# Even heads' row moves through GpSimd's queue for twenty steps, batch 0's attention result kept in float32, and a row tile cleared by ScalarE

## The chip, the cores and the metric

The kernel runs on one core of one Trainium2 chip. The metric is the time of one execution in device microseconds. The engines are called as the profile calls them: PE is TensorE (matrix products; PEld is its weight load), DVE is VectorE, ACT is ScalarE, POOL is GpSimd, and SP is SyncE, which issues transfers. ACT and POOL can issue transfers too; a queue with a q (SPq, ACTq) is the issuing side.

## The reference

Attention with a mix over the heads before and after the softmax, then two feed-forward blocks. All in float32.

```python
batch, n_heads, seq, head_dim = (4, 12, 448, 64)
scores = scale * np.matmul(q, k.transpose(0, 1, 3, 2))
scores = np.einsum('bhij,hg->bgij', scores, w_pre)        # premix over heads
attn = softmax(scores)                                    # max, exp, sum, divide
attn = np.einsum('bhij,hg->bgij', attn, w_post)           # postmix over heads
x = np.matmul(attn, v)    -> 1792 tokens x 768
h = (x @ w1) * (x @ w2) @ w3 @ w_out                      # first block, d_ff 1024
g = np.maximum(0.01 * (h @ w_in), h @ w_in) @ w_out2      # second block, d_ff 2048
```

## The kernel before

The attention takes the first 360 us or so of the span, the two feed-forward blocks the rest. Each batch is cut into four chunks of queries (120, 120, 120 and 88 of them), and the chunks are worked through in `order`; batch 0 begins with its short chunk. A chunk is six pairs of heads for `qk` (L248) and five or six groups of up to twenty queries for everything behind it; there are 92 groups.

`qk` makes the scores of one pair of heads with queries on the partitions. To mix over heads, heads must be on the partitions: each head's scores are evicted from PSUM to a tile `s` (L260 on DVE, L262 on ACT) and then *moved* by a DMA from SBUF to SBUF (`move`, L274), which deals the 120 partitions to ten partitions (one per query of a block, twelve heads apart) and twelve columns of a row tile `rows_of`, name `sr`. There are three row tiles, used in turn, one per chunk. `premix` (L306) multiplies a row tile by `kpre` into `pm`, so it needs the moves of all twelve heads of its chunk. DVE takes the row maximum `mx` (L316), ACT the exponential `e` with the row sums `sm` (L323), `weigh` scales up to four blocks of `e` by 1/sum (L339: three by POOL, one by DVE; in the last steps L337: three by ACT, one by POOL), `postmix` (L360) writes `po`, DVE transposes it to `ap` (L375), and `av` (L392) multiplies by v into `px`, which ACT copies to `y` (L403). For batches 0 and 1, `y` is split in an upper half (`hi_act`, L72: a copy rounded to float32r) and a lower half (L405, POOL: the difference), and both are stored to `scr`. For batches 2 and 3 `y` is stored in float32 alone.

The loop runs in steps of two groups, k = 0, 2, ... 92, under a manual schedule: each engine takes its instructions in program order. Before the loop, eleven `qk` run early (the whole first chunk and five pairs of the second), with `turn` as filler products on PE. There, even heads are evicted by ACT, but those of odd pairs of the first chunk by DVE; the first chunk's even heads are moved by ACT's queue, everything else by SP's. In step k the pairs of groups ten (later eleven and twelve) ahead are made by `qk`, so the last pair of the second, third and fourth chunk is made in step 0, 6 and 12 and its premix stands at the end of step 2, 8 and 14; from the fifth chunk on there are two or three steps between. SP also issues the loads of q, k and v, in program order with the moves.

The row tiles are cleared once at the start (L151 by DVE, L155 by POOL), since `kpre` has zero rows that meet unused partitions.

The *seam* is a generator of the feed-forward part that the last steps of attention call: it loads the first weights and x (both batches' upper and lower halves, four transfers, L757), converts the first weight tile `wr` to `wc` and its halves `ws` in pieces (L100 to L111), and makes the first products `pm` (L587) while the last `av` still runs. Behind it the feed-forward blocks run on PE without gaps. The lower halves of x come in at the second of each pair of `pm`'s first twelve terms.

Of the kernel before, what the change touches and what calls it, by code (L numbers as in the profile page):

```python
# [22 lines left out]
def attention_moe_kernel(ctx: ExitStack, tc, qt, kt, vt, w_pre, w_post, w1, w2, w3t, w_out, w_in2, w_out2, out):  # L23
# [15 lines left out]
    P = 128  # L39
    JP = 112  # L40
    NJ = S // JP
    IB = 10
    LEAD, AT, SKIP = 10, (16, 20), 4
    CH = qt.shape[-1]
# [7 lines left out]
    while i0 < S:  # L52
# [4 lines left out]
    scr = [  # L57
        dram.tile([2, P, NPAIR, S], F32, name=f"scr_{b}") if b < 2 else dram.tile([P, NPAIR, S], F32, name=f"scr_{b}")
        for b in range(B)
# [58 lines left out]
    def attention(seam):  # L118
        with ExitStack() as es, ExitStack() as left:
# [30 lines left out]
            def constants_load():  # L150
                nc.vector.memset(rows_of[0], 0.0)  # L151
                for t in (kpre, kpost):
                    nc.gpsimd.memset(t, 0.0)
                for i in (1, 2):
                    nc.gpsimd.memset(rows_of[i], 0.0)  # L155
                for n, w in enumerate((w_pre, w_post)):
                    nc.sync.dma_start(out=wrep[:, n, :], in_=w)
# [69 lines left out]
            def qk(b, c, p, early=False):  # L227
# [29 lines left out]
                def out():  # L257
                    for e in range(2):
                        if early and (e or (b, c) == order[0] and p % 2):
                            nc.vector.tensor_copy(t[:m, e, :], pq[e][:m])  # L260
                        else:
                            nc.scalar.activation(out=t[:m, e, :], in_=pq[e][:m], func=ACTF.Copy)  # L262
                    for e in range(2):
                        args = srt[b, c], t[:m, e, :], 2 * p + e
                        move(*args, nc.sync if e or (b, c) != order[0] else nc.scalar)

# [8 lines left out]

            evs, staged = [], []

# [99 lines left out]
            def av(b, c, p):  # L377
# [21 lines left out]
                def out():  # L399
                    hi, lo = (y[:, i, 2 * g:2 * g + 2, :ni] for i in range(2))  # L400
                    if b < 2:
                        hi_act(hi, px[:, :, :ni])
                    nc.scalar.copy(lo.bitcast(F32), px[:, :, :ni])  # L403
                    if b < 2:
                        nc.gpsimd.tensor_tensor(out=lo, in0=lo.bitcast(F32), in1=hi.bitcast(F32), op=ALU.subtract)  # L405
# [3 lines left out]
                if p == NPAIR - 1:  # L409
                    if b < 2:  # L410
                        later.extend((scr[b][i, :, :, c0:c0 + ni], y[:, i, :, :ni].bitcast(F32)) for i in range(2))
# [85 lines left out]
            for k in range(0, NG + 2, 2):  # L497
# [8 lines left out]
                before = ets.pop(k - 2, None)  # L506
                ahead = [x for g in made[k] for x in slot(g)]
                for x in ahead:
                    qk(*x)
# [14 lines left out]
                if drain:  # L524
                    if old:
                        turns = postmix(old, before, now=False)
                        turn_out(turns.pop(0))
                    if k > LAST:
                        next(seam, None)
                    if now:  # L530
                        weigh(fresh, sm, ets[k], True)
                    while turns:
                        turn_out(turns.pop(0))
                else:
                    weigh(fresh, sm, ets[k], False)
                while lows:
                    lows.pop(0)()
# [26 lines left out]
    def moe():  # L564
# [66 lines left out]
        def first_half():  # L631
            with ExitStack() as er:
# [112 lines left out]
                def seam():  # L745
# [8 lines left out]
                    pos[0] += 1  # L754
                    for n in range(2):
                        for i in range(2):
                            nc.sync.dma_start(out=x[:, :, i, n * S:(n + 1) * S].bitcast(F32), in_=scr[n][i])  # L757
                    fill()
                    yield
                    steps = converting(cv, loaded.pop(0), (KM, P))  # L760
# [3 lines left out]
                    next(steps)  # L764
                    yield
                    try:
# [5 lines left out]
                    hi_act(w[:, 0], cf)  # L772
                    yield
                    lo_dve(w[:, 1], cf, w[:, 0])
# [347 lines left out]
```

## Time and profile before

| | us |
|---|---|
| three runs | 3006.95, 1218.69, 1223.53 |
| median | 1223.53 |
| profiled execution | 1220.24 |
| its span, first to last instruction | 1218.5 |
| mean granted clock of PE | 0.997 |

The page gives, for the span, the busy time of each engine, the busy share in forty slices, the chain of work that ended last, the costliest groups of instructions and the transfers. A clock of 1.00 is PE's upper level, 2.4 GHz; less is a mean over a stretch that was partly at 1.2 GHz. DMA share is the mean over the core's 16 DMA engines. A number in square brackets with an arrow is the time that an engine was idle before an instruction, and what ended it; where the wait was for several things, only one is named, and not always the right one.

### The profile page before, as it was taken

The numbers are of one execution on the slowest core, as the hardware profiler recorded it, in microseconds if no ns is written. First come the engines' busy times: TensorE is split into PE (matmuls) and PEld (weight loads), VectorE is DVE, ScalarE is ACT, GpSimd is POOL, SyncE is SP. The second block draws the span as 40 slices with busy tenths as digits, with TensorE's granted clock in tenths as the row PEclk, the third lists the DMA queues.
The fourth block names the chain that finished last, engine by engine and source line by source line (L and its number), as shares of the span: only waits on it lengthen the run. The fifth ranks groups of instructions, "written<-read, shape, count | busy, mean of one in ns | idle before, by whom it ended". The sixth has DMA issues, their size and how long they took to land.

```text
span 1218.5 us, 22377 instructions
## 1 busy us (share of the span) xinstructions
PE 1197.1 (98%) x8782; PEld 985.3 (81%) x8782; DVE 885.8 (73%) x1538; ACT 550.8 (45%) x1120; POOL 206.8 (17%) x160
## 2 busy tenths in 40 slices
PE   8899999999999999999999999999999999999998
PEld 5245555554478999998899999999999999999998
DVE  6677887888889998547795867667776657376572
ACT  3677777766755454323454342352233433322120
POOL 4566767666310000000000000000000000000000
PEclk9999999999999999999999999999999999999999
DMA  6876776756957756489674636063242221212012
GB/s 212 222 201 192 211 231 183 221 168 184 300 160 256 238 187 198 162 275 352 221 238 145 216 96 208 26 221 115 92 129 70 65 70 52 72 33 72 26 53 91
DMA packets 134282, 196.81 MB, mean 162 GB/s; under 512 B 26304, under 2 KB 114976, under 8 KB 134176
## 3 DMA queue, kind: packets, MB, share of 16 engines
q1 hardware_dynamic: 129656, 192.77, 49.7%
q10 hardware_dynamic: 4520, 2.61, 0.7%
q8 instruction: 69, 1.13, 0.4%
q14 instruction: 37, 0.30, 0.1%
HBM read 114.57 MB, written 42.07 MB: 129 GB/s over the span
## 4 chain that ended last, share of the span: by engine, by line
PE 82%; DVE 8%; DMA 5%; ACT 3%; issue 1%; ACTq 0%; SPq 0%; POOL 0%; DVEq 0%; POOLq 0%
PE pm L587 29%; PE po L601 19%; PE pp L898 17%; DVE ap L375 6%; PE pw L659 6%; PE px L392 5%; PE po L360 3%; ACT e L323 3%; DMA sr<-s 3%; PE pq L248 2%; DVE mx L316 1%; DMA x<-scr 1%; PE pm L306 1%; DMA q<-in_q_dram 1%; PE turn L293 1%
## 5 line engine op out<-in xcount | busy, mean ns | idle before, releaser
L587 PE MATMUL pm<-x,ws 128*128 128x384 f32 (+1 forms) x1152 | 233.9, 364 | 0.0
L587 PEld LDWEIGHTS pm<-x,ws 128*128 128x128 f32 x1152 | 208.7, 188 | 24.5 <-issue 0.6
L339 POOL TENSOR_SCALAR e<-e,sm 128x448 f32<-128x448 f32 x126 | 181.9, 1456 | 141.0 <-DVE sm L333 123.1
L323 ACT ACTIVATE e<-pm,mx 128x448 f32<-128x448 f32 x180 | 111.7, 632 | 85.3 <-DVE mx L316 80.8
L375 DVE STREAM_TRANSPOSE ap<-po 128x512 f32<-128x512 f32 (+3 forms) x228 | 116.7, 571 | 25.2 <-PE po L360 24.5
L898 PE MATMUL pp<-t,w 128*128 128x448 f32 x576 | 124.5, 368 | 0.0
L601 PE MATMUL po<-ws,g 128*128 128x384 f32 x672 | 117.2, 334 | 0.0
L601 PE MATMUL po<-wo,g 128*128 128x384 f32 x672 | 117.1, 334 | 0.0
L898 PEld LDWEIGHTS pp<-t,w 128*128 128x128 f32 x576 | 108.1, 188 | 10.9
L601 PEld LDWEIGHTS po<-wo,g 128*128 128x128 f32 x672 | 116.6, 188 | 0.2
L601 PEld LDWEIGHTS po<-ws,g 128*128 128x128 f32 x672 | 116.6, 188 | 0.0
L316 DVE TENSOR_REDUCE mx<-pm 128x1 f32<-128x448 f32 x180 | 98.5, 603 | 11.7 <-PE pm L306 11.7
L100 ACT ACTIVATE wc<-wr 128x768 f32<-128x768 f32 (+1 forms) x72 | 61.6, 858 | 85.0 <-DMA wr<-in_moe_w_dram 29.1
L392 PEld LDWEIGHTS px<-ap,vs 96*64 96x64 f32 (+1 forms) x1536 | 77.7, 136 | 22.1 <-ACT e L323 16.7
L898 PE MATMUL pp<-b,w 128*128 128x448 f32 x432 | 95.5, 368 | 0.0
L608 DVE TENSOR_TENSOR acc<-po,acc 128x384 f32<-128x384 f32 x84 | 45.5, 555 | 66.5 <-PE po L601 66.4
L306 PE MATMUL pm<-sr,kpre 64*64 64x448 f32 x720 | 82.0, 555 | 9.0 <-DMA sr<-s 4.8
L392 PE MATMUL px<-ap,vs 96*64 96x120 f32 (+3 forms) x1536 | 87.6, 266 | 2.9 <-ACT e L323 1.0
L360 PE MATMUL po<-e,kpost 64*32 64x512 f32 (+1 forms) x1472 | 89.1, 586 | 0.8 <-POOL e L339 0.7
L262 ACT ACTIVATE s<-pq 120x448 f32<-120x448 f32 (+1 forms) x178 | 82.2, 563 | 12.7 <-PE pq L248 10.9
L898 PEld LDWEIGHTS pp<-b,w 128*128 128x128 f32 x432 | 81.1, 188 | 8.0
L248 PEld LDWEIGHTS pq<-k,q 64*120 64x120 f32 (+1 forms) x528 | 44.6, 176 | 46.9 <-DVE ap L375 17.6
(104 smaller groups left out, 1580.9 us busy)
## 6 DMA issues: line engine op xcount, KB each, us to landing
sr<-s SPq DMA_DIRECT2D x144, 210.0 KB
wr<-in_moe_w_out_dram SPq DMA_DIRECT2D x24, 768.0 KB
wr<-in_moe_w_dram SPq DMA_DIRECT2D x16, 768.0 KB
wr<-in_moe_w_in_dram SPq DMA_DIRECT2D x16, 768.0 KB
wr<-in_moe_w_dram SPq DMA_DIRECT2D x16, 512.0 KB
sr<-s SPq DMA_DIRECT2D x42, 157.5 KB
vs<-in_v_dram SPq DMA_DIRECT2D x12, 512.0 KB
kept_w<-wc SPq DMA_DIRECT2D x16, 384.0 KB
```

Of the source, the lines that this page charges most:

```text
L262: nc.scalar.activation(out=t[:m, e, :], in_=pq[e][:m], func=ACTF.Copy)
L306: nc.tensor.matmul(pms[ns[s % len(ns)]][half:half + Q], kpre[rows], sr[rows, 2 * t + g, :], start=True, stop=True,)
L316: nc.vector.tensor_reduce(out=mxs[n], in_=pms[n], axis=AX.X, op=ALU.max, negate=True)
L323: ends["act"] = nc.scalar.activation(out=e[:, i], in_=pms.pop(n), func=ACTF.Exp, bias=mxs.pop(n), scale=1.0, accum_out=sm[:, i:i + 1])
L339: ends["dve" if eng is nc.vector else "pool"] = eng.tensor_scalar(out=e[:, i], in0=e[:, i], scalar1=rc[:, i:i + 1], scalar2=None, op0=ALU.mult
L360: nc.tensor.matmul(po[g][32 * r:32 * (r + 1), :m], kpost[rows, x], e[rows, :m, JS[r]:JS[r] + P], start=True, stop=True,)
L375: ends["dve"] = nc.vector.transpose(out=dst, in_=po[g][:, i0:i1])
L392: nc.tensor.matmul(px[e * D:(e + 1) * D, r, :nw].rearrange("p (n i) -> p n i", i=HQ), vs[rows, p, jc, e, :], ap[rows, x, :ns, jc, h * HQ:( ...
L587: nc.tensor.matmul(dst, wt[:, a, kk, :], x[kk][:, c, c0:c0 + w], start=(i == 0), stop=(i == len(steps) - 1))
L601: nc.tensor.matmul(po, g[m][:, a, t * P:(t + 1) * P], wts[m][:, c, cs], start=(m == 0 and j == 0), stop=(m == FQ - 1 and j == 2),)
L659: nc.tensor.matmul(pw, wt[:, x, kk, :], wos[kk][y][:, cs], start=(kk == 0 and j == 0), stop=(kk == KF - 1 and j == 2),)
L898: nc.tensor.matmul(dst, w[:, i, a, kk, :], b[:, kk, c, :], start=(kk == 0 and j == 0), stop=(kk == KH - 1 and j == 2),)
```

## The change

Even heads (e = 0) are always evicted by ACT in the early `qk`, odd ones by DVE. The early even heads are moved by POOL's queue. In the steps below k = 40, twenty of them, the even heads' moves are put on a list and issued by POOL's queue behind its part of `weigh`; odd heads stay on SP, and from step 40 on SP moves all. Batch 0's `y` is stored once in float32; at the seam it is loaded into the place of x's lower half, ACT copies it to the upper half in three pieces of 2 x 448 columns (two in the step of group 88, one in the next), and POOL subtracts behind its `weigh`. One of the two row tiles that POOL cleared is cleared by ACT, as a copy of the zeroed `kpre`.

```diff
-    LEAD, AT, SKIP = 10, (16, 20), 4
+    LEAD, AT, SOFT, SKIP = 10, (16, 20), 40, 4
...
-        dram.tile([2, P, NPAIR, S], ...) if b < 2 else dram.tile([P, NPAIR, S], ...)
+        dram.tile([2, P, NPAIR, S], ...) if b == 1 else dram.tile([P, NPAIR, S], ...)
...
-                for i in (1, 2):
-                    nc.gpsimd.memset(rows_of[i], 0.0)
+                nc.gpsimd.memset(rows_of[1], 0.0)
+                none = rows_of[2].rearrange("p n s -> p (n s)").rearrange("p (a b) -> p a b", b=Q)
+                nc.scalar.activation(
+                    out=none, in_=kpre.unsqueeze(1).to_broadcast([P, CH // IB * S // Q, Q]), func=ACTF.Copy
+                )
...
-                        if early and (e or (b, c) == order[0] and p % 2):
+                        if early and e:
                             nc.vector.tensor_copy(t[:m, e, :], pq[e][:m])
                         else:
                             nc.scalar.activation(out=t[:m, e, :], in_=pq[e][:m], func=ACTF.Copy)
                     for e in range(2):
                         args = srt[b, c], t[:m, e, :], 2 * p + e
-                        move(*args, nc.sync if e or (b, c) != order[0] else nc.scalar)
+                        if early or e or not soft[0]:
+                            move(*args, nc.sync if e or not early else nc.gpsimd)
+                        else:
+                            soon.append(args)
...
-                    if b < 2:
+                    if b == 1:
                         hi_act(hi, px[:, :, :ni])
                     nc.scalar.copy(lo.bitcast(F32), px[:, :, :ni])
-                    if b < 2:
+                    if b == 1:
                         nc.gpsimd.tensor_tensor(out=lo, in0=lo.bitcast(F32), in1=hi.bitcast(F32), op=ALU.subtract)
...
+                soft[0] = k < SOFT
...
-                    if k > LAST:
-                        next(seam, None)
+                    rest = next(seam, None) if k > LAST else None
                     if now:
                         weigh(fresh, sm, ets[k], True)
+                    if rest:
+                        rest()
...
                     weigh(fresh, sm, ets[k], False)
+                    while soon:
+                        move(*soon.pop(0), nc.gpsimd)
...
-                    for n in range(2):
-                        for i in range(2):
-                            nc.sync.dma_start(out=x[:, :, i, n * S:(n + 1) * S].bitcast(F32), in_=scr[n][i])
+                    for i, c0, src in ((1, 0, scr[0]), (0, S, scr[1][0]), (1, S, scr[1][1])):
+                        nc.sync.dma_start(out=x[:, :, i, c0:c0 + S].bitcast(F32), in_=src)
                     fill()
+                    def halves(*ks):
+                        hi, lo = ([x[:, k:k + 2, i, :S] for k in ks] for i in range(2))
+                        for y, z in zip(hi, lo):
+                            hi_act(y, z.bitcast(F32))
+                        def rest():
+                            for y, z in zip(hi, lo):
+                                nc.gpsimd.tensor_tensor(
+                                    out=z, in0=z.bitcast(F32), in1=y.bitcast(F32), op=ALU.subtract
+                                )
+                        return rest
                     yield
...
                     next(steps)
-                    yield
+                    yield halves(0, 2)
+                    rest = halves(4)
...
                     hi_act(w[:, 0], cf)
-                    yield
+                    yield rest
                     lo_dve(w[:, 1], cf, w[:, 0])
```

## Rows read from the trace of the kernel before

**Rows 1.** Stages: window, us, busy us (instructions) per engine, clock, DMA share, GB/s

```profile
84.00:312.00 228.00, 223.73 (x2990) 121.18 (x2992) 184.51 (x401) 165.89 (x466) 150.64 (x116) 1.00 0.69 199
38.00:42.00 4.00, 4.00 (x31) 1.40 (x39) 1.48 (x4) 3.03 (x8) 1.38 (x1) 0.64 0.92 217
80.00:84.00 4.00, 2.09 (x10) 0.72 (x12) 2.07 (x5) 1.34 (x4) 2.77 (x3) 0.73 0.66 196
```

**Rows 2.** Timeline of PE, first 84 us: start, us, what, [idle before, what ended it]

```profile
16.57 1.02 PE L248 MATMUL pq<-k,q 64*120 64x448 f32 x4 [0.69 <-ACT s L262]
21.32 1.73 PE L306 MATMUL pm<-sr,kpre 64*64 64x448 f32 x16 [2.19 <-DMA sr<-s]
25.03 1.02 PE L248 MATMUL pq<-k,q 64*120 64x448 f32 x4 [1.03 <-DMA q<-in_q_dram]
36.81 1.15 PE L306 MATMUL pm<-sr,kpre 64*64 64x448 f32 x8 [2.57 <-DMA sr<-s]
59.04 1.09 PE L306 MATMUL pm<-sr,kpre 64*64 64x448 f32 x8 [2.21 <-DMA vs<-in_v_dram]
81.91 1.88 PE L306 MATMUL pm<-sr,kpre 64*64 64x448 f32 x8 [2.00 <-DMA q<-in_q_dram]
```

**Rows 3.** DMA queues from 13 to 19 us: packets, MB, share of 16 engines

```profile
q10 hardware_dynamic: 414, 0.67, 33.6%
q1 hardware_dynamic: 346, 0.56, 29.4%
```

**Rows 4.** Timeline of the start: POOL's clears, ACT's and SP's issues

```profile
1.40 9.10 POOL L155 MEMSET sr<- 128x5376 f32 x2
...
8.45 2.31 ACTq L274 DMA_DIRECT2D sr<-s  x2
8.58 10.43 SPq L274 DMA_DIRECT2D sr<-s  x8
...
19.06 1.81 SPq L205 DMA_DIRECT2D q<-in_q_dram  x2
```

**Rows 5.** Tile sr, 20 to 90 us: SP's issues, ns min/median/max, first and last start

```profile
L274 SPq DMA_DIRECT2D sr<-s x42: 755/756/995, 21.0 to 89.9; - x42
```

**Rows 6.** Groups of POOL by form: busy us, mean ns, idle before

```profile
L339 POOL TENSOR_SCALAR e<-e,sm 128x448 f32<-128x448 f32 x126 | 181.9, 1456 | 141.0 <-DVE sm L333 123.1 <-ACT s L262 18.0
L405 POOL TENSOR_TENSOR y<-y 128x240 fp32r<-128x240 f32 x18 | 12.4, 690 | 0.0
L405 POOL TENSOR_TENSOR y<-y 128x176 fp32r<-128x176 f32 x6 | 3.3, 555 | 0.0
```

**Rows 7.** Timeline of POOL: weigh of steps 0, 16 and 38

```profile
26.15 4.34 POOL L339 TENSOR_SCALAR e<-e,sm 128x448 f32<-128x448 f32 x3 [15.66 <-ACT s L262]
...
86.36 4.34 POOL L339 TENSOR_SCALAR e<-e,sm 128x448 f32<-128x448 f32 x3 [3.59 <-DVE sm L333]
...
169.45 2.97 POOL L339 TENSOR_SCALAR e<-e,sm 128x448 f32<-128x448 f32 x2 [2.21 <-DVE sm L333]
```

**Rows 8.** Groups of ACT by form, attention: its copies of q and k

```profile
L72 ACT ACTIVATE q<-q 128x360 fp32r<-128x360 f32 x24 | 13.6, 568 | 0.8 <-DMA q<-in_q_dram 0.8
L72 ACT ACTIVATE k<-k 128x896 fp32r<-128x896 f32 x9 | 8.9, 987 | 1.8 <-DMA k<-in_k_dram 1.8
```

**Rows 9.** Timeline of the seam, all engines

```profile
341.19 1.79 ACT L337 ACTIVATE e<-e,sm 128x448 f32<-128x448 f32 x3 [1.29 <-DVE sm L333]
...
343.07 2.07 PE L360 MATMUL po<-e,kpost 64*32 64x512 f32 x32
...
346.54 0.84 ACT L72 ACTIVATE ws<-wc 128x768 fp32r<-128x768 f32 x1 [1.47 <-DVE wc L111]
...
350.14 7.55 PE L587 MATMUL pm<-x,ws 128*128 128x512 f32 x36
```

**Rows 10.** Chain that ended last, 265 to 365 us: the load of x

```profile
316.82 15.01 DMA x<-scr
```

**Rows 11.** Groups of DVE by form, attention: its share of weigh

```profile
L339 DVE TENSOR_SCALAR e<-e,sm 128x448 f32<-128x448 f32 x37 | 16.8, 453 | 1.4
```

More of the change, by code (lines that the diff above doesn't have):

```diff
@@ L57, in attention_moe_kernel @@
     scr = [
-        dram.tile([2, P, NPAIR, S], F32, name=f"scr_{b}") if b < 2 else dram.tile([P, NPAIR, S], F32, name=f"scr_{b}")
+        dram.tile([2, P, NPAIR, S], F32, name=f"scr_{b}") if b == 1 else dram.tile([P, NPAIR, S], F32, name=f"scr_{b}")
         for b in range(B)
@@ L274, in move @@
                 ends["sync"] = queue.dma_start(out=dst[SKIP + h:SKIP + h + H * (IB - 1) + 1:H, :w, :], in_=t)
-            evs, staged = [], []
+            evs, staged, soon, soft = [], [], [], [True]
             def evict():
@@ L409, in av @@
                 if p == NPAIR - 1:
-                    if b < 2:
+                    if b == 1:
                         later.extend((scr[b][i, :, :, c0:c0 + ni], y[:, i, :, :ni].bitcast(F32)) for i in range(2))
```

## The prediction

> **What bounds the kernel now.** I read the page first: its list of busy times and its forty slices show TensorE filled in nearly every slice, so nothing can be won under it; only its own idle time and its slow stretches are to be had. The table of stages puts numbers on it: from 84 to 312 us TensorE is busy 223.73 of 228 us at the full granted clock, and the stretches that differ lie before, where the clock falls to 0.64 and 0.73 of full speed, that is partly to the lower of its two levels, 1.2 GHz [rows 1]. TensorE's own timeline then names the idle times of the first 84 us and what ended each [rows 2]: 0.69, 2.19, 1.03, 2.57, 2.21 and 2.00 us, 10.69 us in all. Four of the six stand before `pm` (L306), the premix, which needs all twelve heads' moves of its chunk. The clock falls behind two of them: 38 to 42 us is granted 0.64, which loses 0.36 x 4 = 1.44 us, and 80 to 84 us 0.73, which loses 1.08 us [rows 1]. So 13.2 us are lost to late data in the first 84 us, and that is all that this change can reach: 1.1% of the time.
>
> Why the data is late is in the queues' views. Between 13 and 19 us almost only moves run; the two hardware queues then hold 33.6% and 29.4% of the 16 DMA engines, 63% together [rows 3]. From 38 to 42 us, with loads among them, the share is 0.92 [rows 1]. 63% is close to 10/16, and the destination of a move has ten partitions per column: I read it as moves that keep ten engines full and leave six idle. SP and ACT meanwhile issue for long: eight moves in 10.43 us on SP, two in 2.31 us on ACT, where evictions queue behind them, and the q loads of the third chunk only at 19.06 us, behind those eight [rows 4].
>
> The Trainium skill ("DMA: Bandwidth & Descriptors", section "Why a DMA increments its semaphore by 16 and not by 1") says that a transfer is split over the largest number up to 16 that divides the slowest dimension of both sides, here ten, and that the hardware path takes the lowest-numbered engines, while GpSimd's software path takes consecutive ones from a cursor that goes round, or all 16. The 63% agrees for the hardware path; no row here has a move from GpSimd.
>
> **The change, part by part.** *Even heads' moves by GpSimd, before the steps.* Eleven even moves leave ACT and SP. ACT no longer stops for 2.31 us between evictions, and SP reaches the q loads behind seven moves in place of eight, none of which waits for ACT. GpSimd's price for one issue is not in the trace. The lower bound is SP's fastest issue of the same move, 0.755 us [rows 5]; the upper one GpSimd's dearest instruction in a step, 1.456 us [rows 6]. I take 1.1 us, the middle, which is also about ACT's 2.31/2. Six even moves of the first chunk from 8.45 us then end at 15.1 us, with their transfers in a third queue. Of the 0.69 + 2.19 us of idleness I count 2.4 us as won, of the 1.03 us for q 1.0 us.
>
> *Even heads' moves by GpSimd, in the first twenty steps.* They go out behind the three `weigh` instructions, so 3 x 1.456 us = 4.35 us plus 1.1 us after `weigh` begins. Where does that matter? The last pair of a chunk is moved only one step ahead of its premix for the second, third and fourth chunk (steps 0, 6 and 12; the waits at 36.81, 59.04 and 81.91 us [rows 2]), and two or more steps ahead from the fifth on, where no such wait is seen. For the wait at 36.81: `weigh` of step 0 began at 26.15 us [rows 7], would begin 3.4 us earlier (the two gains above) at 22.75, end at 27.1, the first issue at 28.2; with 2.5 us to land (an estimate: the moves of [rows 3], 1.23 MB of them in 6 us, take about 1 us each, and I add as much again and a half for the queue) the data is there at 30.7 us, when TensorE arrives, at 36.81 - 2.57 - 3.4 = 30.8 us. Of 2.57 + 1.44 I count 2.7 us. The later two lie among the loads of k, q and v, behind which the odd heads still queue on SP: half, 1.1 us of 2.21, and 1.6 us of 2.00 + 1.08. Sum of the gains: 2.4 + 1.0 + 2.7 + 1.1 + 1.6 = 8.8 us.
>
> *GpSimd's own load.* In a step it has 4.35 us of `weigh` and now two issues, 6.55 us with 1.1 us each. From 86.36 to 169.45 us `weigh` begins eleven steps in 83.1 us, 7.55 us a step: it fits, cost 0. From 26.15 to 86.36 us there are eight steps in 60.2 us; less the three waits and the lost clock, 9.3 us, that is 6.4 us a step [rows 7, 1, 2]. There GpSimd is 0.15 us a step too long, 1.2 us over eight; some of it can be carried where the reader of `weigh`'s result comes later, so I count 0.5 us. At 1.456 us an issue the eight steps give back 8 x 0.86 = 6.9 us; at 0.755 us nothing.
>
> *Batch 0's y in float32.* Twelve ACT copies and twelve GpSimd subtractions (0.690 and 0.555 us [rows 6]) go, with four stores and one load of x. All lay beside TensorE's work: gain 0, though it makes room on GpSimd from 55 us on. Added are three ACT copies and three subtractions of 896 columns at the end. ACT's price is the 0.987 us of its 128 x 896 row [rows 8]; GpSimd's, from 555 ns at 176 and 690 ns at 240 columns, is 2.1 ns a column, 2.07 us each. Two copies stand ahead of `weigh` in the step at 337 us: ACT was idle for 1.29 us before it began `weigh` at 341.19 [rows 9], so from 339.90; two copies end at 341.87, `weigh` moves back by 0.7 us, and so does the `po` at 343.07, which began right behind ACT's last scaling (341.19 + 1.79 = 342.98). The third copy fits in the 1.47 us before `ws` at 346.54. GpSimd's subtractions run from about 343.4 to 347.5 and, behind its next `weigh`, from 349 to 351; the first product begins at 350.14 [rows 9] and comes to the last pair of x's lower halves in its second microsecond. Cost 0.7 us. The x that they split had landed by 316.82 + 15.01 = 331.83 us [rows 10], and there is less of it now.
>
> *ACT clears a row tile.* 5,376 columns by the two rows of [rows 8]: slope (987 - 568)/536 = 0.78 ns, 4.5 us; at the whole 896-column row's rate, 5.9 us. ACT has nothing before the first eviction, which ends at its first issue, 8.45 us, and the tile is wanted chunks later: 0. GpSimd's two clears ran from 1.40 to 10.50 us [rows 4]; one less frees it near 6 us, and it needs to be free, for its first move at 8.45 us.
>
> Sum: -8.8 + 0.5 + 0.7 = -7.6 us. The profiled execution took 1220.24 us (span 1218.5 and 1.7 around it): 1213 us. It lies between the two lower runs shown, 1218.69 and 1223.53; the median is the slower of these, so the same gain against the median would read 1216.
>
> **The rivals.** *Little is won (0.20).* The moves are as many bytes; if GpSimd's also sit on the ten full engines, the even heads only change places with the odd ones, and of [rows 2] only the first and third wait and half of the second go, which stem from the order on ACT and SP: 2.8 us, less 1.2 and about a microsecond of later landings: 1218 to 1221 us. For it: 63% came from two queues together [rows 3]. Against it: with six engines idle a third queue may find them. The Trainium skill has this too (same page, "Issuing engines are not separate DMA queues": only issuing time is saved), and the two queues at 63% do not contradict it.
>
> *GpSimd becomes the bound (0.18), the one on the other side.* Place: its queue in the first twenty steps, 4.35 us plus two issues against 6.4 us (eight steps) and 7.55 us (twelve). An issue of d us costs 8 x (2d - 2.05) us and, above 1.6 us, 12 x (2d - 3.2) us more. It cancels the gains near 1.53 us. At 1.75 us it costs 15.2 us: 1227 us. At 2.0 us, 25.2 us: 1237 us. From 2.2 us on the kernel is slower by over 2%. For it: no issue by GpSimd is in the trace, and with 1.456 us for 448 columns it is the slowest engine. Against: issuing works by rows, not by columns.
>
> *The port (0.07).* VectorE scales one block a step from SBUF to SBUF, 0.453 us x 37 [rows 11]; `weigh`, issues and subtractions could wait for it, or hold up VectorE's weight conversion at the seam. Price: up to one subtraction, 2.07 us, at the conversion that releases `ws` [rows 9], and 20 x 0.45 us on GpSimd, of which twelve steps hide theirs: 8 x 0.45 = 3.6 us: 1215 to 1219 us. The Trainium skill ("SBUF — State Buffer", section "Who interferes with whom") states such a lock between VectorE and GpSimd and says that it stalls the descriptors of GpSimd's transfers; no row here shows GpSimd writing descriptors.
>
> **How the numbers follow.** The forecast, waits cut by about two thirds, has 0.55: 1207 us if all 13.2 us come back less 0.7, 1217 us if a third does. The others have 0.20, 0.18 and 0.07. The range 1206 to 1228 us holds the first, second and fourth, and of the third what lies below 1.75 us an issue, together a little over 0.8. Two per cent, about what a measurement of this kernel can tell from no change, is 24 us: faster by that has 0.01, since there are not 24 us to win; slower 0.05, an issue above 2.2 us; within it 0.94.
>
> **What would show it.** Right: TensorE's idle times at 21, 25, 37, 59 and 82 us shorter, the clock at 1.00 there, the mean DMA share above 0.63 in 13 to 19 us, GpSimd's issues near 1.1 us each, and the seam's first product near 343 us in place of 350. Wrong: `po` waiting for GpSimd's `e` in the first twenty steps (its price too low), the waits before `pm` unchanged with GpSimd idle (the bytes bind), or a gain at 84 us that is gone at the seam (`po` waiting for ACT, or `ws` late).

## The result and the profile after

The changed kernel takes 1228.73 us (median of six runs, 1228.49 to 1230.25) against 1221.57 us for the kernel before in the same session: 1.0073 times as long, 95% interval 1.0045 to 1.0102 (the ratio leaves out the first of the three runs of before, 3006.95 us, which the median counts). It is slower by 0.7%, less than 2%; 1213 was predicted, and the range ended at 1228. The profiled execution took 1228.67 us, span 1226.4, mean granted clock 0.994.

TensorE's timeline, where the late data shows, as in [rows 2]:

```profile
26.49 3.07 PE L312 MATMUL pm<-sr,kpre 64*64 64x448 f32 x16 [9.01 <-DMA sr<-s]
40.71 0.98 PE L312 MATMUL pm<-sr,kpre 64*64 64x448 f32 x8 [1.24 <-issue]
65.98 1.77 PE L312 MATMUL pm<-sr,kpre 64*64 64x448 f32 x8 [6.56 <-DMA sr<-s]
89.88 0.98 PE L312 MATMUL pm<-sr,kpre 64*64 64x448 f32 x8 [1.13 <-DMA sr<-s]
```

The second chunk's wait went from 2.57 to 1.24 us, as forecast, though in a loop that begins 6 us late. But the first premix waits 9.01 us in place of 2.19, the third chunk's 6.56 in place of 2.21. The stage from 13 to 19 us in the kernel before (columns as in [rows 1]):

```profile
13.00:19.00 6.00, 5.30 (x32) 2.82 (x28) 5.08 (x16) 2.83 (x6) 0.00 (x0) 1.00 0.63 204
```

The same stage and another in the changed kernel:

```profile
13.00:19.00 6.00, 4.48 (x28) 2.54 (x24) 3.94 (x13) 2.69 (x5) 3.50 (x6) 1.00 0.86 208
84.00:312.00 228.00, 222.88 (x2990) 120.46 (x2992) 188.47 (x406) 164.11 (x459) 164.07 (x139) 1.00 0.69 193
```

The queues from 13 to 19 us (columns as in [rows 3]):

```profile
q0 software_dynamic: 313, 0.82, 59.8%
q1 hardware_dynamic: 263, 0.43, 26.2%
```

q0 is GpSimd's queue. The share rose from 63% [rows 3] to 86%, as forecast, and the bytes did not follow: 208 GB/s against 204. GpSimd's queue took 0.82 MB of it, and SP's came down from 0.56 MB [rows 3] to 0.43. GpSimd's group of issues, up to 130 us:

```profile
L280 POOL DMA_DIRECT2D sr<-s x39 | 23.5, 604 | 4.7 <-DVE s L263 2.1 <-ACT s L265 1.4 <-issue 1.1
```

Its timeline, steps 6, 8 and 10, and step 16:

```profile
50.88 4.34 POOL L345 TENSOR_SCALAR e<-e,sm 128x448 f32<-128x448 f32 x3 [1.18 <-DVE sm L339]
55.17 1.21 POOL L280 DMA_DIRECT2D sr<-s  x2
57.59 4.34 POOL L345 TENSOR_SCALAR e<-e,sm 128x448 f32<-128x448 f32 x3 [1.21 <-DVE sm L339]
61.88 1.21 POOL L280 DMA_DIRECT2D sr<-s  x2
70.86 4.34 POOL L345 TENSOR_SCALAR e<-e,sm 128x448 f32<-128x448 f32 x3 [7.77 <-DVE sm L339]
...
93.56 4.34 POOL L345 TENSOR_SCALAR e<-e,sm 128x448 f32<-128x448 f32 x3 [1.44 <-DVE sm L339]
```

SP's timeline of the start:

```profile
7.89 10.46 SPq L280 DMA_DIRECT2D sr<-s  x7
18.40 5.15 SPq L208 DMA_DIRECT2D q<-in_q_dram  x2
```

An issue by GpSimd costs 0.604 us, and GpSimd is never the bound: from step 2 to step 38 it is idle before each `weigh`, for 0.4 us at the least and 7.77 at the most. SP's seven moves take as long as its eight did [rows 4], and it then stands 5.15 us over two loads of q, where it stood 1.81. The issues of the start are not late, though. GpSimd's sixth, the last even head of the first chunk, ends at 13.66 us, where ACT's last ended at 15.93; SP's seven end at 18.35, where its eight ended at 19.01. The first premix begins 5.2 us later all the same, so what holds it up is the transfers and not the evictions or the issues. ACT's timeline of the start in the kernel before, and GpSimd's in the changed one:

```profile
13.66 2.27 ACTq L274 DMA_DIRECT2D sr<-s  x2
```

```profile
13.06 0.60 POOL L280 DMA_DIRECT2D sr<-s  x1 [0.15 <-issue]
```

The difference of the two spans, 7.99 us, lies so (`weigh` of step 0, step 16, the first drain step, and the first product): 6.06 us up to step 0 (32.21 against 26.15), 1.14 us from there to step 16 (93.56, against 86.36 [rows 7]), -0.52 us to the drain (324.48 against 317.80), 1.08 us in the seam (first product 357.90 against 350.14 [rows 9]), 0.23 us behind it. The seam, timeline of all engines:

```profile
346.49 1.79 ACT L72 ACTIVATE x<-x 128x896 fp32r<-128x896 f32 x2
349.37 4.16 POOL L777 TENSOR_TENSOR x<-x 128x896 fp32r<-128x896 f32 x2
350.05 2.07 PE L366 MATMUL po<-e,kpost 64*32 64x512 f32 x32 [0.41 <-issue]
352.57 1.77 DVE L111 SCALAR_TENSOR_TENSOR wc<-wr,wc 128x768 uint32<-128x768 uint32 x1
354.27 0.15 DVE L337 TENSOR_SCALAR sm<-sm 128x3 f32<-128x3 f32 x1
354.83 1.40 POOL L345 TENSOR_SCALAR e<-e,sm 128x448 f32<-128x448 f32 x1 [1.30 <-DVE sm L339]
356.44 1.52 PE L366 MATMUL po<-e,kpost 64*32 64x384 f32 x32 [0.71 <-POOL e L345]
```

In the kernel before, VectorE's conversion stood there so:

```profile
345.59 0.92 DVE L111 SCALAR_TENSOR_TENSOR wc<-wr,wc 128x768 uint32<-128x768 uint32 x1
```

### The profile page after: what moved, and what is told of

It reads as the page before. It is cut to its first block, busy times and chain, and to the rows that moved or that the text cites. A ratio compares the mean times of both kernels' runs of the same rounds, so it can differ in the third digit from the quotient of the medians.

```text
span 1226.4 us, 22376 instructions
## 1 busy us (share of the span) xinstructions
PE 1196.1 (98%) x8782; PEld 984.3 (80%) x8782; DVE 886.5 (72%) x1535; ACT 557.4 (45%) x1115; POOL 233.1 (19%) x204
## 4 chain that ended last, share of the span: by engine, by line
PE 83%; DVE 8%; ACT 3%; DMA 3%; issue 1%; POOL 1%; ACTq 0%; POOLq 0%; SPq 0%; DVEq 0%
PE pm L597 29%; PE po L611 19%; PE pp L923 17%; DVE ap L381 6%; PE pw L669 6%; PE px L398 5%; PE po L366 4%; DMA sr<-s 3%; ACT e L329 3%; PE pm L312 2%; PE pq L251 2%; DVE mx L322 1%; PE turn L299 1%; POOL e L345 1%; POOL sr L280 0%
## 5 line engine op out<-in xcount | busy, mean ns | idle before, releaser
L923 PEld LDWEIGHTS pp<-t,w 128*128 128x128 f32 x576 | 108.1, 188 | 10.9
L312 PEld LDWEIGHTS pm<-sr,kpre 64*64 64x64 f32 x720 | 24.6, 134 | 75.9 <-issue 33.4
```

What stands on the lines that cost most here:

```text
L312: nc.tensor.matmul(pms[ns[s % len(ns)]][half:half + Q], kpre[rows], sr[rows, 2 * t + g, :], start=True, stop=True,)
L923: nc.tensor.matmul(dst, w[:, i, a, kk, :], b[:, kk, c, :], start=(kk == 0 and j == 0), stop=(kk == KH - 1 and j == 2),)
```

## The experiments

"Ratio" is to the kernel before in the same session, with its 95% interval.

| run | median us | ratio |
|---|---|---|
| e1 second chunk's even heads on SP | 1227.37 | 1.0059 [1.0039, 1.0080] |
| e2 start as before | 1223.81 | 1.0031 [1.0009, 1.0054] |
| e3 steps as before | 1221.77 | 1.0023 [0.9997, 1.0049] |
| e4 the y part alone | 1220.61 | 1.0008 [0.9978, 1.0039] |
| e5 GpSimd's moves ahead of weigh | 1224.42 | 1.0048 [1.0029, 1.0067] |
| e6 the steps' late moves on SP | 1224.26 | 1.0057 [1.0039, 1.0074] |
| e7 the kernel before again | 1218.51 | 1.0003 [0.9976, 1.0030] |
| e8 start as before, ahead of weigh | 1223.86 | 1.0032 [1.0008, 1.0056] |
| e9 kernel before, plain rows | 1208.51 | 0.9904 [0.9874, 0.9934] |
| e10 steps on ScalarE, early | 1221.63 | 1.0012 [0.9991, 1.0034] |
| e11 steps on ScalarE, late | 1225.61 | 1.0053 [1.0027, 1.0079] |
| e12 plain rows, eleven engines | 1208.58 | 0.9921 [0.9893, 0.9949] |
| e13 the change on plain rows | 1216.49 | 0.9973 [0.9952, 0.9993] |
| e14 all early moves on GpSimd | 1225.74 | 1.0041 [1.0017, 1.0065] |
| e15 kernel before, loads behind moves | 1235.08 | 1.0103 [1.0064, 1.0142] |
| e16 changed kernel, loads behind moves | 1230.88 | 1.0102 [1.0085, 1.0119] |

**Which part costs (e2, e3, e4, e7).** e2 has the early evictions and moves of before; e3 has `SOFT = 0`, so that no step uses GpSimd's queue; e4 is the kernel before with the y part of the diff alone; e7 is the kernel before.

```diff
-    LEAD, AT, SOFT, SKIP = 10, (16, 20), 40, 4      # e3
+    LEAD, AT, SOFT, SKIP = 10, (16, 20), 0, 4
...
-  move(*args, nc.sync if e or not early else nc.gpsimd)      # e2
+  move(*args, nc.scalar if early and not e and (b, c) == order[0] else nc.sync)
```

> The changed kernel with the moves and evictions before the steps as in the kernel before (ACT's queue for the first chunk's even heads, SP for the rest); the steps' even heads stay on GpSimd behind weigh. Theory A: the whole loss at the start, 6 us at weigh of step 0, goes; step 6 is then ahead of the kernel before by 2 to 4 us, the premix in step 8 still waits over 4 us, and the kernel ends within 2 us of the kernel before, seam included: 1220 to 1224 us. Rival (moves by GpSimd in the steps are what costs): weigh of step 16 is still 5 us or more behind the kernel before and the time 1226 or more.

> The changed kernel with SOFT = 0: in the steps SP moves all heads as before; before the steps GpSimd moves the even heads. Theory A: the 6 us of the start stay (weigh of step 0 near 32.2 us), the waits in the steps are those of the kernel before or shorter, and with 1.1 us at the seam the time is 1225 to 1229 us. Rival (the steps cost): weigh of step 16 less than 3 us behind the kernel before, 1221 to 1223 us.

> The kernel before with one part of the change: batch 0's y stored once in float32 and split at the seam. Theory: start and steps as in the kernel before, first product of the feed-forward part 1.1 us later (351.2 us for 350.14): VectorE's second conversion under GpSimd's subtraction takes 1.8 us in place of 0.9 and ACT's copies stand before weigh; 1221 to 1224 us. Rival (what the part saves in transfers and in GpSimd's and ACT's steps is worth as much): no difference or up to 2 us faster.

> The kernel before, once more, for a second profile: the variant with the y part alone showed a premix wait of 5.39 us at 61.5 us where the kernel before showed 2.21 us, and its start differed by 0.6 us although the program is the same there. If the waits of the first 90 us vary from one execution to the next, this profile shows other waits at 37, 59 and 82 us than 2.57, 2.21 and 2.00 us, and weigh of step 16 anywhere from 85 to 91 us; if they belong to the program, it shows the same to 0.3 us, and the difference of the y part is its own.

No part alone costs what all cost. The ratios less one, 0.8 per mille for y, 1.5 more with the start and the clear (e3 less e4), 2.3 more with the steps (e2 less e4), add up to 4.6 against 7.3 for the whole; with intervals of some 2.5 each, that the rest comes of the parts together is likely but not shown, nor is the order of the three. The y part is the one that the traces single out: from `weigh` of the first drain step to the first product it is 32.34 and 32.35 us in both profiles of the kernel before, and 33.38 in e4. e3 was expected at 1225 to 1229 us and missed. Its waits before the premixes, TensorE's timeline:

```profile
26.37 3.16 PE L312 MATMUL pm<-sr,kpre 64*64 64x448 f32 x16 [8.87 <-DMA sr<-s]
60.75 0.98 PE L312 MATMUL pm<-sr,kpre 64*64 64x448 f32 x8 [1.83 <-DMA sr<-s]
```

The start is as bad as in the changed kernel, and it does not matter: `weigh` of step 0 begins 6.0 us later than in [rows 7], that of step 16 at 86.17, 0.2 us earlier. With the moves of the steps on SP, the later chunks' waits shrink by what the first one grew. In e2 the start is good (step 0 at 25.20), and the third chunk's premix waits 6.76 us at 61.59. So a late start is paid back while the steps run on SP. That the steps on GpSimd cost by themselves is likely (e2's ratio is above 1 clear of its interval, but the y part is in it), not shown. e7 and e4 add a caution: the kernel before has waits of 2.77 and 2.64 us at 36.61 and 59.26 and none near 82 when it is profiled again, and e4, the same up to the seam, has 2.52 at 37.76 and 5.39 at 61.51. In e7 `weigh` of step 16 begins at 84.80 us, in e4 at 89.82. So a single wait is in part a matter of the execution, and one profile against one proves little; the times of the kernel before reach from 1212 to 1228 us over these sessions, those of the changed one from 1228.5 to 1230.3.

**Whose order (e1).** Only the first chunk's even heads on GpSimd at the start, the second's on SP.

```diff
-  move(*args, nc.sync if e or not early else nc.gpsimd)
+  move(*args, nc.gpsimd if early and not e and (b, c) == order[0] else nc.sync)
```

> The changed kernel, but before the steps only the first chunk's even heads go by GpSimd's queue; the second chunk's five even heads go by SP. In the changed kernel TensorE stands 9.01 us before its first premix (26.49 us), while both queues together move some 200 GB/s, no more than the two hardware queues of the kernel before. Theory A (fixed rate, wrong order): the second chunk's even heads took the bytes that the first chunk's odd heads needed; with them behind on SP the first premix begins at 19 to 21.5 us, its wait is under 3 us, and the kernel is 4 to 6 us faster than the changed one, about 1223 us. Rival B (the software path holds up SP's transfers whatever it carries): the wait stays above 6 us and the time within 2 us of the changed kernel's 1228.7.

TensorE's timeline:

```profile
22.59 3.26 PE L312 MATMUL pm<-sr,kpre 64*64 64x448 f32 x16 [5.75 <-DMA q<-in_q_dram]
```

The first premix waits 5.75 us in place of 9.01, outside the 8.87 to 11.97 us of the five profiles whose start is that of the changed kernel (it, e3, e5, e6, e16), and not under 3 as expected. That order explains a part, about 3 us of wait, and little of the time, as e3 says it must. The rest, some 3 us over the kernel before, stays open; in e1 the two queues move 178 GB/s from 13 to 19 us, less than ACT's and SP's did.

**Late or slow (e5, e6, e8, e10, e11).** In the steps the moves leave behind `weigh`. e5 puts them ahead of it; e8 does so with the start of before. e6 issues them from SP at the place behind `weigh`; e10 and e11, with the start of before, from ScalarE behind the eviction, or at the end of the step.

```diff
+                    while soon:                                   # e5, e8
+                        move(*soon.pop(0), nc.gpsimd)
                     weigh(fresh, sm, ets[k], False)
-                    while soon:
-                        move(*soon.pop(0), nc.gpsimd)             # e6: nc.sync
...
-                            soon.append(args)                     # e10
+                            move(*args, nc.scalar)
...
                 do(k // 2, upper)
+                while soon:                                       # e11
+                    move(*soon.pop(0), nc.scalar)
```

> The changed kernel with the even heads' moves issued by GpSimd ahead of its part of weigh in place of behind it, so 4.3 us earlier in each of the twenty steps; everything else as changed. Theory L (they leave too late, behind the loads of k and v that SP now reaches sooner): the premix wait at 66 us (6.56 us) falls under 3.5 us and the time to 1222 to 1225 us; the 9 us at the start stay. Rival P (a transfer of GpSimd's queue lands late, 9 to 11 us, whenever k and v are loaded, wherever it stands): the wait stays above 5 us and the time within 2 us of 1228.7.

> The changed kernel with the even heads' moves at the same place of the step, behind weigh and behind that step's odd heads, but issued by SP, so that they also stand behind some of the loads; before the steps as changed. Theory L (the place is what costs): the premix wait at 66 us stays above 5 us and the time is 1226 to 1229 us. Rival P (GpSimd's path is what costs): the wait falls under 3.5 us and the time to that of the variant with SP moving all heads in the steps, 1222 us.

> Start as in the kernel before and, in the steps, even heads on GpSimd ahead of weigh. Theory L: with neither the lost start nor the late issue, the premix waits at 37 and 60 us are under 2 us each, weigh of step 16 is 1 to 4 us ahead of the kernel before, and the time is 1217 to 1220 us in spite of the seam's 1 us. Rival P: as the variant with the old start and the moves behind weigh, 1223 to 1225 us.

> The changed kernel with the start as before, and in the first twenty steps the even heads' moves issued by ScalarE's queue right behind the eviction, in place of GpSimd's queue behind its weigh. Theory L (GpSimd's moves hurt because they leave late, behind weigh): the premix of the third chunk waits under 3 us in place of 6.76, the first drain step's weigh begins at 315 to 318 us, 1219 to 1221 us. Theory Q (GpSimd's queue itself lands late among the loads, whenever it is issued): the same numbers as L here; the next run tells them apart. A third: ScalarE's issues (two of 1.1 us a step) delay its evictions or exponentials, the step grows by up to 1 us over the first eight steps: 1224 to 1230 us.

> As the run before, but ScalarE issues the even heads' moves at the end of its step, so as late as GpSimd did or later. Theory L (lateness): the premix of the third chunk waits 5 to 8 us again, the first drain step's weigh begins at 319 to 321 us, 1223 to 1225 us. Theory Q (GpSimd's queue itself): under 3 us of wait, 315 to 318 us, 1219 to 1221 us.

e5, TensorE's timeline:

```profile
39.42 1.95 PE L366 MATMUL po<-e,kpost 64*32 64x512 f32 x32 [0.42 <-POOL e L345]
46.25 1.95 PE L366 MATMUL po<-e,kpost 64*32 64x512 f32 x32 [1.53 <-POOL e L345]
52.15 1.91 PE L366 MATMUL po<-e,kpost 64*32 64x384 f32 x32 [0.59 <-POOL e L345]
63.73 0.98 PE L312 MATMUL pm<-sr,kpre 64*64 64x448 f32 x8 [1.30 <-DMA sr<-s]
```

Four microseconds earlier, and the third chunk's wait is 1.30 in place of 6.56 us. Behind `weigh` it is 5.72 to 6.76 us in four profiles (the changed kernel, e1, e2, e14), ahead of it 1.30 and 3.72 in two (e5, e8), so leaving late is its likely cause, though e4 shows 5.39 with SP alone. But now `po` waits for GpSimd's scaling in three steps, and little is won. e8 gives the same exchange (`po` waits 1.37 us at 33.45), and its time is the rival's, not the 1217 to 1220 us expected. e10, early on ScalarE, waits 2.38 us for `e` at 61.82, and is within 0.3% of the kernel before (its profile is of its slowest execution, 1226.17 us); e11, late on ScalarE, waits 1.33 us there, and loses in other places, where `px` waits 3.38 and 1.96 us for ScalarE's `e` behind its issues. So the waits of this chunk do not follow the late leaving alone (e11 was expected at 5 to 8 us and missed), and the theory that GpSimd's queue is slow by itself is not shown either: on GpSimd and, late, on ScalarE these issues hold up something that stands behind them on the same engine. e6 does not test the place: SP does not wait for `weigh`, so the moves left right behind the odd ones, ahead of the loads. The third chunk then waits 2.15 us, as the rival had it; the time is 1224.26 us, not its 1222.

**Why a third queue brings no bytes (e9, e12, e14).** e9 writes each move to the same-numbered partitions; e12 does this with 110 of 120 rows (88 of 90); both leave out the dealing. e14 is the changed kernel with all early moves on GpSimd's queue.

```diff
-  ... queue.dma_start(out=dst[SKIP + h:SKIP + h + H * (IB - 1) + 1:H, :w, :], in_=t)
+  n = t.shape[0]                  # e12: n = t.shape[0] // 11 * 11
+  ... queue.dma_start(out=dst[:n, h, :], in_=t[:n])
...
-  move(*args, nc.sync if e or not early else nc.gpsimd)       # e14
+  move(*args, nc.gpsimd if early else nc.sync)
```

> The kernel before, but every move writes one head's 120 (or 90) partitions to the same-numbered partitions of the row tile's column, in place of dealing them to ten partitions; the dealing of queries to partitions is left out, bytes and number of moves are the same. Theory T (ten destination partitions keep ten engines full and leave six idle, the prediction's reading of the 63%): the two queues now reach a share above 0.8 and over 280 GB/s in 13 to 19 us, the first premix waits less than 0.5 us (2.19 to 2.70 before), and the waits of the third and fourth chunk shrink below 1 us: 1212 to 1216 us. Theory R (the moves run at a rate of about 200 GB/s whichever engines hold them): 190 to 230 GB/s in 13 to 19 us, the waits of the kernel before stay within their scatter, 1217 to 1222 us.

> The run with plain rows, but each move carries 110 (88) of the head's 120 (90) rows, 11 times 10 (8), so that the split over engines comes out at eleven in place of fifteen; the dealing and the last rows are left out. Theory T (the number of engines that a move is split over binds): the first move alone has 11 packets in flight in place of 15, the rate in 13 to 19 us falls back to 205 to 225 GB/s, and the premixes wait again (first or second over 1 us): 1211 to 1219 us. Theory D (what binds is that the rows are dealt to ten destination partitions): like the run with plain rows, 240 GB/s or more, no premix waits over 0.5 us, 1207 to 1211 us.

> The changed kernel, but before the steps GpSimd issues the odd heads' moves too, so that its queue is alone with the moves there. Theory S (its queue reaches all sixteen engines, move after move): above 235 GB/s in 12 to 20 us, more than 13 packets in flight, and the first premix waits less than the 9 us of the changed kernel. Theory T (every move sits on the same ten engines, whoever issues it): about ten packets in flight and 195 to 210 GB/s; issue order is the program's again, so the first premix waits 2 to 5 us and the evictions are not held up: 1225 to 1229 us.

The queue's row while one early move runs alone, in the kernel before (10.2 to 10.6 us):

```profile
q10 hardware_dynamic: 42, 0.08, 62.0%
```

In the changed kernel (9.6 to 10.0 us), with GpSimd's first move:

```profile
q0 software_dynamic: 23, 0.08, 60.5%
```

In e9 (9.4 to 9.8 us):

```profile
q10 hardware_dynamic: 52, 0.09, 86.8%
```

The share is packet time over 16 engines, so sixteen times it is the mean number of packets under way: 9.9, 9.7 and 13.9. A dealt move has ten, on GpSimd's queue as well; a plain one has about fourteen. The Trainium skill ("DMA: Bandwidth & Descriptors", section "Why a DMA increments its semaphore by 16 and not by 1") gives a transfer the largest number of engines up to 16 that divides both slowest dimensions, 10 and 15 here; the first two rows agree, and 13.9 lies nearer to 15 than to 10. Two stages of e9:

```profile
13.00:19.00 6.00, 5.64 (x40) 2.96 (x40) 4.24 (x14) 2.37 (x6) 0.00 (x0) 1.00 0.88 247
38.00:84.00 46.00, 43.24 (x560) 21.83 (x564) 37.99 (x85) 35.64 (x100) 30.10 (x24) 1.00 0.93 249
```

One of e12:

```profile
13.00:19.00 6.00, 5.68 (x38) 3.00 (x38) 4.61 (x15) 2.58 (x6) 0.00 (x0) 1.00 0.73 209
```

And of e14:

```profile
13.00:19.00 6.00, 5.21 (x32) 2.91 (x28) 4.54 (x14) 3.21 (x6) 4.63 (x9) 1.00 0.87 194
```

Split over fifteen, the moves run at 247 GB/s (over 280 was expected), no premix waits over 0.4 us, and 1% is won; over eleven, at 209. So the shape of a move sets the rate. e9 changes two things, the number of engines and the number of partitions written, and e12, which writes 110 partitions and falls back to 209, speaks for the engines. The time does not tell e12 from e9: it is as fast, with 8% fewer bytes and eleven engines, and no premix waits 0.3 us or more, so what freed its premixes at this rate stays open. e14 is the run against the prediction: GpSimd's queue alone, move behind move, shows the share of 0.87 that full engines would, and 194 GB/s; its first premix waits 5.54 us. From 16 to 22 us its row shows 93.0% and 1.14 MB in 6 us, 189 GB/s. A share that rises with no more bytes is packets that stand longer, not idle engines put to work. The trace does not tell the engine of a packet, so whether six engines stand idle or all sixteen run slower on such rows is open; that GpSimd's queue does not get more out of them is shown.

**The change where the engines do not bind (e13).** The changed kernel with e9's edit.

> The changed kernel with plain rows (the dealing is left out). Theory E (the change's loss before the seam is that a third queue shares the ten engines): with fifteen engines the first premix waits under 2 us in place of 9, the third chunk's under 2 in place of 6.6, and the run is within 4 us of the kernel before with plain rows, 1208 to 1213 us, the rest being the seam's microsecond. Theory G (GpSimd's queue is slow by itself, whatever the engines): the first premix still waits over 5 us or the third chunk's over 4: 1214 to 1220 us.

No premix waits for its moves over 0.4 us, as expected, yet 1216.49 us lies in the other theory's range: 8 us over e9's median (5.7 us from span to span), as much as the change costs on dealt rows. The place is another. TensorE's timeline of e13:

```profile
25.09 1.85 PE L251 MATMUL pq<-k,q 64*120 64x448 f32 x4 [5.15 <-DMA q<-in_q_dram]
```

Its stage from 19 to 28 us:

```profile
19.00:28.00 9.00, 3.85 (x13) 1.85 (x14) 2.32 (x6) 4.38 (x12) 5.02 (x5) 0.67 0.96 266
```

TensorE waits 5.15 us for the third chunk's q, the clock falls to 0.67 there, and `weigh` of step 2 begins 5.8 us behind e9's (34.7 against 28.9); at step 16 it is 4.5 us (80.6 against 76.1) and 1 us more comes in the seam. The steps with GpSimd's issues cost nothing here. So their price on dealt rows looks to be that of the lower rate, and the start has a second price, SP's late q, which on dealt rows may hide behind the late moves. How GpSimd's moves wait is seen in the queues, too. In e13 it issues two at 51.03 us; from 51 to 53 us only SP's queue has a row:

```profile
q1 hardware_dynamic: 176, 0.56, 96.7%
```

In the changed kernel, from 56 to 58 us, behind the two issues at 55.17:

```profile
q1 hardware_dynamic: 193, 0.41, 103.8%
q0 software_dynamic: 3, 0.01, 1.5%
```

Tile `sr` of the changed kernel, the issues from 55 to 56 us:

```profile
DMA to landing us min/median/max: 10.6/10.9/11.1
```

While SP's queue has transfers in hand GpSimd's moves hardly start, and they land 10.9 us after their issue; in e13, where SP's queue drains faster (0.56 MB in 2 us against 0.41), it is 5.5 us. That they stand behind SP's backlog fits both, but is not shown. The prediction's rival "The port" names another way: VectorE holding up GpSimd's issues. VectorE's timeline of the changed kernel:

```profile
57.02 0.17 DVE L337 TENSOR_SCALAR sm<-sm 128x4 f32<-128x4 f32 x1 [1.18 <-ACT e L329]
```

VectorE was idle for the 1.18 us up to 57.02 us, while GpSimd's queue moved next to nothing, so that way does not explain this stretch.

**Loads behind moves (e15, e16).** Each step's loads of k and q behind that step's moves on SP.

```diff
-                for job in (k_load, q_load):
-                    do(k // 2, job)
...
                 evict()
+                for job in (k_load, q_load):
+                    do(k // 2, job)
```

> The kernel before, with each step's loads of k and q issued by SP behind that step's moves in place of ahead of them. Theory O (in the first 84 us the bytes bind, and what a load gets ahead of a move is what the premix waits for): the premix of the second and third chunk waits under 1.5 us each (2.57 to 2.77 and 2.21 to 2.64 before), weigh of step 16 begins at 82 to 84 us, 1215 to 1218 us. Against it: the loads land a few us later and ScalarE's conversion of k waits for them, up to 2 us a step: 1220 to 1226 us.

> The changed kernel, with each step's loads of k and q issued by SP behind that step's odd moves. Theory O (GpSimd's moves, issued behind weigh, stand behind loads that SP has issued meanwhile): the third chunk's premix waits at most 3 us in place of 6.6, weigh of step 16 begins at 87 to 90 us in place of 93.6, 1222 to 1225 us. Theory G (GpSimd's queue lands late whatever SP has issued): 6 to 7 us of wait again, 1227 to 1230 us.

Both are slower, outside every range expected. In e15 the second chunk's wait is gone, but the third chunk's premix waits 3.35 us at 57.20, and most is lost behind the first 84 us: `qk` waits 3.09 us for ScalarE at 105.47 and 4.65 at 155.09, and from step 16 to the first drain step it is 243.3 us, where the kernel before takes 230.3 or 231.4. In e16 the third chunk waits 5.18 us for ScalarE's conversion of k. So the loads are urgent too. e16 was meant to show whether the loads are what GpSimd's moves stand behind, and does not: its moves still take 9.3 and 10.2 us to land at 59.0 us.

## Why the prediction was wrong

*The step that failed* is "moves that keep ten engines full and leave six idle", used as if a third queue would fill the six. Its first half held: ten packets under way on one move, and split over fifteen the waits go (e9). The second half fell: GpSimd's move of the same shape also has ten (60.5%), and the rate stays at 208 GB/s with a share of 0.86 in the changed kernel and at 189 to 194 with 0.87 to 0.93 in e14 (204 before). Whether six engines stay idle or all run slower is open; a third queue added nothing either way. The rival "Little is won" stated this mechanism and had 0.20; its time, 1218 to 1221, was too low as well, because it priced a third queue at a microsecond of later landings.

*The even heads at the start* were to win 3.4 us and lost 6 at step 0. Two things were not costed. At a rate that does not rise, the second chunk's even heads, issued early by a free queue, take bytes from the first chunk's odd heads: SP's queue moved 0.43 MB where it moved 0.56, and e1 gives 3 us of the wait back. And SP was done with its two q loads at 23.55 us, not before 20.87. Neither shows in the time while the later waits shrink in return (e3): the waits of the first 84 us were not separate losses to be added up, as the 13.2 us had them. In e9, at the higher rate, all the premix waits go together. Two of the four premix waits in [rows 2] also name a load and not a move, and that at 82 us is not there when the kernel before is profiled again.

*The steps.* The issue price was mis-sized, 0.604 us and not 1.1, below the lower bound of 0.755: GpSimd's issue could not be costed by SP's. That helped, and the rival "GpSimd becomes the bound" did not come about. The term that mattered was the 2.5 us to land: it is 3.8 to 4.4 us at step 0 and 10.6 to 11.1 at step 6. For the second chunk's wait (2.57 to 1.24) the reasoning held but for this; the third, counted as +1.1, came to -4.35.

*The seam* was to cost 0.7 and costs 1.08, most of it at another place. ScalarE's two copies took 1.79 us, the `po` behind them waited 0.41, and it begins 0.3 us later against the drain step than before (25.57 us behind it, 25.27 before). The other 0.8 us is the rival "The port": VectorE's conversion L111, 0.92 us long in the kernel before, both times, takes 1.77 where it meets GpSimd's subtraction (349.37 to 353.53), and everything behind it, `sm`, `weigh` and `po`, is late by that. It ends 0.81 us after the subtraction, and so it does in e1, e2, e3 and e14, though it takes 1.62 to 2.07 us there: it waited for it. The Trainium skill ("SBUF — State Buffer", section "Who interferes with whom") says that a VectorE instruction with two SBUF inputs contends with a GpSimd one that reads SBUF; L111 reads `wr` and `wc`, and these rows agree. Other terms held: the clear 4.68 us (4.5), a subtraction 2.08 us (2.07), a copy 0.90 (0.99).

*The range* missed by 0.7 us: its upper end came from a GpSimd that is too slow, which was not what happened, so that the miss is small is luck. Its lower end, 1207 us, is 1207.7 by its own terms.

## What to carry to other kernels

A DMA share is packets under way, not engines at work; before a third queue is counted on to fill the rest, look whether the bytes rise with the share, and when several waits come from one rate, count the bytes rather than the waits. An issue that moves to another engine is placed behind that engine's compute and in front of it at once: price what it waits for, what waits for it, and the backlog that the freed queue gets ahead of it. Of these moves from SBUF to SBUF, the shape of the side with the fewer partitions was worth more than the choice of the queue (247 against 204 GB/s).

## What was not expected of the hardware

GpSimd issues a move of 120 rows of 1,792 bytes in 0.604 us, less than SP's 0.755, and its queue sends the bytes in fewer packets (23 on 0.08 MB, nine of them under 512 bytes, against 42): by that about three rows to a packet, which may be why it took two thirds of the bytes beside SP's queue. Its transfers land 2.8 us after the first issue of the start, and 10.9 us where SP's queue had transfers in hand. The kernel before scatters by 16 us between executions. Its two profiles, 2.7 us apart, differ by 1.6 us up to step 16, where the waits are, and by 1.2 us from there to the drain. That second stretch takes nearly the same time in many variants, 230.2 to 231.4 us from `weigh` of step 16 to that of the first drain step in the kernel before, both profiles, the changed one, e3, e9 and e13; e15 has 243.3.
